# A decode layer on one core: w_down, gate and up dealt over the partitions in another way

## The chip, the core and the metric

The kernel runs on one core of one Trainium2 chip. The metric is the device time of one execution in microseconds (us), the median of several runs. The profile shows one execution on the same chip: what each engine did, what it waited for, and what the DMA queues moved. Engines are called as in the profile: PE is TensorE, DVE is VectorE, ACT is ScalarE, POOL is GpSimd and SP is SyncE. "PEld" is the loading of weights into PE, and "SPq" or "POOLq" is the sequencer of an engine that issues transfers.

## The reference

One token passes a layer norm, and its normalised row feeds attention over a cache of 16384 positions in 32 heads and a gated feed-forward block; both results are added to the token. All is float32.

```python
def _A_ref(x, k_cache, v_cache, wq, wo):
    q = (x @ wq).reshape(B, Sq, H, Dh) ...
    scores = einsum("bhqd,bhkd->bhqk", q, k_cache) * (Dh ** -0.5)
    o = einsum("bhqk,bhkd->bhqd", softmax(scores), v_cache)
    return o ... @ wo

def _B_ref(x, w_gate, w_up, w_down):
    h = gelu(x @ w_gate) * (x @ w_up)
    return h @ w_down

xn = layernorm(x)
return x + _A_ref(xn, ...) + _B_ref(xn, ...)
```

## The kernel before

Nearly all the work is reading: two caches of 268 MB each and 51 MB of weights. SBUF holds three slots of 64 KB a partition: two for keys (`kslot`, lines 62 to 63) and one for values (`vslot`, lines 65 to 66). Every weight and cache tile passes through one of them, and a load waits until the former content of its slot has been used. All loads but those of the token are issued by SP with `load` (lines 68 to 70), in the order of the program.

**Start.** SP loads wq, the fourth rows and the tails of gate and up (lines 74 to 80), then the main part of gate, later that of up (line 169). The token's row is normalised and turned into columns (lines 82 to 126). `project` (lines 128 to 141) multiplies it with a weight matrix: the columns of the result are cut into four quarters, quarter q goes to partitions 32q to 32q+31 of PSUM, and each quarter is cut again into pieces of at most 512 columns, a PSUM bank each. For gate and up a quarter has 4608 / 4 = 1152 columns in pieces of 396, 396 and 360. Each of the five steps (four groups of 128 input rows and a tail of 64 rows) is 12 matmuls. The last 64 input rows lie in halves: the first 2304 columns in one set of partitions, the others in the other.

`ffn` (lines 165 to 179) then brings the result to where w_down needs it: DVE multiplies each piece with `same`, which keeps for every partition the one block of columns that belongs to it, and a reduction adds the blocks. Partition p ends with the 36 values of gate (and of up) that stand for the rows 36p to 36p+35 of w_down. `ffn_act` (lines 186 to 196) makes hT from them, 36 values a partition.

**Heads.** For each head SP loads one tile of keys and one of values (8.4 MB each, 64 KB a partition). DVE multiplies keys by the query and reduces (lines 210 to 216), a softmax follows, and PE multiplies the weights with the values (lines 232 to 237).

**End.** w_down (`wd`) lies with 36 rows a partition, wo with 32. SP loads 28 rows of wd into the value slot when the last but one head's values have been used, 8 rows into the key slot that comes free next together with 16 rows of wo, and 8, 4, 2, 1 and 1 rows of wo into the last slot (lines 287 to 297). A "row" here is 2304 bytes in each of 128 partitions. PE multiplies each row, 288 columns at a time, with one column of hT or oT (`add_out`, lines 278 to 282, called from lines 312 to 325). wd rows come first, then wo rows in the order of their loads. Ahead of the last four wo rows DVE adds the partial sums to the token (lines 320 and 321), PE adds that in (line 324), and after the last row DVE copies the result and ACT stores it (lines 327 to 329).

GpSimd has only a few memsets and an identity matrix at the start and issues no transfer.

Of the kernel before, what the change touches and what calls it, by code (L numbers as in the profile page):

```python
# [19 lines left out]
DM = P * DJ  # L20
# [15 lines left out]
HG = 4  # L36
# [5 lines left out]
def kernel(ctx: ExitStack, tc: tile.TileContext, x, k_cache, v_cache, wq, wo, wg, wu, wd, out):  # L42
    nc = tc.nc
    cpool = ctx.enter_context(tc.tile_pool(name="cpool", bufs=1))
# [12 lines left out]
    wmain = {n: w[:DM].rearrange("(p j) f -> p (j f)", j=DJ) for n, w in (("q", wq), ("g", wg), ("u", wu))}  # L57
    wtail = {n: w[DM:].rearrange("d (s f) -> (d s) f", s=2) for n, w in (("q", wq), ("g", wg), ("u", wu))}
    wov = wo.rearrange("(p t) f -> p (t f)", t=WO_T)
    wdv = wd.rearrange("(p t) f -> p (t f)", t=WD_T)  # L60

    def kslot():
        return kpool.tile([P, R * DH], F32, tag="k", name="kslot")

    def vslot():
        return vpool.tile([P, R * DH], F32, tag="v", name="vslot")

    def load(dst, src):
        nc.sync.dma_start(dst, src)  # L69
# [9 lines left out]
        tails[n] = load(mix[:, at + DF : at + DF + DF // 2], wtail[n])  # L79
        at += DF + DF // 2  # L80

    xrow = mix[:1, ROW3 + FG : ROW3 + FG + D]
    nc.scalar.dma_start(xrow, xf)
    x2 = cpool.tile([P, HALF], F32, name="x2")
    nc.gpsimd.memset(x2, 0.0)
# [11 lines left out]
    same = cpool.tile([P, 32], F32, name="same")  # L97
# [18 lines left out]
    xd = mix[:1, ROW3 + 2 * FG : ROW3 + 2 * FG + 2 * (D - DM)].rearrange("o (d s) -> o d s", s=2)  # L116
# [4 lines left out]
    xnb = cpool.tile([P, DJ, 32], F32, name="xnb")  # L121
# [3 lines left out]
    xtb = cpool.tile([P, 2, 32], F32, name="xtb")  # L125
    nc.vector.tensor_copy(xtb, xt.unsqueeze(2).to_broadcast([P, 2, 32]))

    def project(steps, group, sizes):
        pg = ps_big.tile([P, 3, 512], F32, tag="pb", name="pg")
        for k, (j, rhs) in enumerate(steps):  # L130
            for b, size in enumerate(sizes):
                for q in range(4):
                    lo = q * group + sum(sizes[:b])
                    if j < DJ:
                        lhs = xnb[:, j, :]
                    else:
                        lhs = xtb[:, q // 2, :]
                        lo -= q // 2 * 2 * group
                    nc.tensor.matmul(pg[32 * q : 32 * q + 32, b, :size], lhs, rhs[:, lo : lo + size],  # L139
                                     start=k == 0, stop=k == len(steps) - 1)  # L140
        return pg

    steps = [(DJ, qt)] + [(j, wq_t[:, j * HD : (j + 1) * HD]) for j in range(DJ)]
    pq = project(steps, QG, (QB, QB))[:, :2, :]
# [5 lines left out]
    def q_spread(h):  # L150
        r = 32 * (h // (H // 4))
        lo = h % (H // 4) * DH
        pq = ps_s.tile([P, 512], F32, tag="sm", name="pq")
        nc.tensor.matmul(pq, ones[r : r + 1, :], qrow[r : r + 1, lo : lo + QH * DH], start=True, stop=True)  # L154
        return pq
# [4 lines left out]
        for i in range(QH):  # L160
            Q[h + i] = qs[:, i : i + 1, :]

    gu = cpool.tile([P, 2, WD_T], F32, name="gu")

    def ffn(which):
        n = "gu"[which]
        t = kslot() if which else wg_t
        steps = [(3, row3[n]), (DJ, tails[n])]
        load(t[:, :ROW3], wmain[n][:, :ROW3])
        steps += [(j, t[:, j * DF : (j + 1) * DF]) for j in range(DJ - 1)]  # L170
        pg = project(steps, FG, FB)
        gm = mix[:, ROW3 : ROW3 + FG].rearrange("p (m t) -> p m t", t=WD_T)
        at = 0
        for b, size in enumerate(FB):
            m = size // WD_T
            nc.vector.tensor_mul(gm[:, at : at + m, :], pg[:, b, :size].rearrange("p (m t) -> p m t", t=WD_T),  # L176
                                 same[:, at : at + m].unsqueeze(2).to_broadcast([P, m, WD_T]))
            at += m
        nc.vector.tensor_reduce(gu[:, which, :], gm.rearrange("p m t -> p t m"), axis=AX.X, op=ALU.add)  # L179

    ffn(0)
    ffn(1)

    hT = cpool.tile([P, WD_T], F32, name="hT")

    def ffn_act():
        g, u = gu[:, 0], gu[:, 1]
        t1 = cpool.tile([P, WD_T], F32, name="t1")
# [3 lines left out]
        th = cpool.tile([P, WD_T], F32, name="th")  # L192
        nc.scalar.activation(th, t1, AF.Tanh, scale=0.7978845608028654)
        t2 = cpool.tile([P, WD_T], F32, name="t2")
# [54 lines left out]
    for h in range(H + 1):  # L249
# [7 lines left out]
        pq = q_spread(h + 1) if more else None  # L257
# [20 lines left out]
    def add_out(groups, lhs, w, last=False):  # L278
        n = D // len(groups)
        for i, g in enumerate(groups):  # L280
            nc.tensor.matmul(g, lhs, w[:, i * n : (i + 1) * n], start=id(g) not in seen, stop=last)  # L281
# [29 lines left out]

    for j, w in enumerate(wd_rows):
        add_out(half[j % 2], hT[:, j : j + 1], w)

    for j, w in enumerate(wo_rows):
        if j < WO_T - WO_Q:
# [2 lines left out]
        if j == WO_T - 4:  # L319
            nc.vector.tensor_add(x2[:64], x2[:64], PO[0][64:, :HALF])  # L320
# [37 lines left out]
```

## Time and profile before

| | |
|---|---|
| time, median of 3 runs | 1370.0 us (1369.81 to 1370.03) |
| time of the profiled execution | 1370.16 us |
| its span, first to last instruction | 1368.3 us |
| bytes read | 587.60 MB, 429 GB/s over the span |
| busy share | DVE 83%, PE 30%, PE weight loads 9%, ACT 3%, POOL 0% |
| PE's granted clock, mean | 0.623 of full speed |

The profile's page cuts the span into 40 slices and gives a busy share for each engine and for the 16 DMA engines, lists the DMA queues, follows the chain of work that ended last back to its start, and lists groups of instructions with the busy time, the mean duration, and the idle time before them with the name of what ended it. Other views give the same chain in order of time, the instructions of a stretch one by one, and, for windows of one's choice, the busy time of each engine, the granted clock, the mean busy share of the DMA engines and the rate. The DMA views show no single DMA engine, only the mean of the sixteen.

### The profile page before, as it was taken

Reading aid. Unit: us, or ns where it says so; the run is one execution under the profiler, and the core shown is the slowest. Engines: PE = TensorE matmul, PEld = TensorE weight load, DVE = VectorE, ACT = ScalarE, POOL = GpSimd, SP = SyncE. Lnnn points to the kernel's source line nnn. Section 1 sums busy time; section 2 is a strip of 40 time slices with the busy share of each in tenths; the row PEclk is TensorE's granted clock in tenths of the full one; section 3 lists DMA queues with packets and bytes.
Section 4 is the critical chain, followed back from the end, with each engine's and each line's share of the span. In section 5 each row is a group of like instructions: output and inputs, shape, how many; then the busy total and the mean of one; then the engine's idle time right before and its main releaser. Section 6 shows DMA issues by size and latency. Waiting matters only on the chain.

```text
span 1368.3 us, 6377 instructions
## 1 busy us (share of the span) xinstructions
PE 406.0 (30%) x2870; PEld 118.1 (9%) x2870; DVE 1135.8 (83%) x169; ACT 36.5 (3%) x126; POOL 1.0 (0%) x7
## 2 busy tenths in 40 slices
PE   4321233322311232323212332322213333221156
PEld 1110000100000000100000000100001000000012
DVE  1069999899888888898888888998888888988840
ACT  0000000000000000000000000000000000000000
POOL 0000000000000000000000000000000000000000
PEclk8775565565556556565566566565556555665577
DMA  9999999999999999999999999999999999999997
GB/s 404 440 425 450 430 429 430 430 435 432 437 435 429 431 430 439 432 432 435 431 436 433 433 431 430 435 432 439 435 430 430 431 432 437 438 435 428 429 428 336
DMA packets 11704, 588.00 MB, mean 430 GB/s; under 512 B 1303, under 2 KB 1309, under 8 KB 1694
## 3 DMA queue, kind: packets, MB, share of 16 engines
q1 hardware_dynamic: 11664, 587.60, 99.4%
q8 instruction: 22, 0.36, 0.1%
q14 instruction: 4, 0.03, 0.0%
q10 hardware_dynamic: 14, 0.01, 0.0%
HBM read 587.60 MB, written 0.00 MB: 429 GB/s over the span
## 4 chain that ended last, share of the span: by engine, by line
DMA 51%; DVE 46%; PE 2%; issue 0%; SPq 0%; ACT 0%; DVEq 0%
DMA kslot<-in_A_k_cache_dram 41%; DVE s L216 23%; DVE kslot L215 23%; DMA kslot<-in_A_v_cache_dram 3%; DMA kslot<-in_B_w_up_dram 3%; DMA kslot<-in_A_wo_dram 3%; DMA kslot<-in_A_wq_dram 2%; PE pg L139 1%; PE po L236 1%; DVE gu L179 0%; SPq L69 0%; PE pt L222 0%; DVE vslot L176 0%; DVE pm L220 0%; DVE nm L224 0%
## 5 line engine op out<-in xcount | busy, mean ns | idle before, releaser
L215 DVE TENSOR_TENSOR kslot<-kslot,qs 128x16384 f32<-128x16384 f32 (+1 forms) x33 | 551.3, 16705 | 88.4 <-DMA kslot<-in_A_k_cache_dram 86.9
L216 DVE TENSOR_REDUCE s<-kslot 128x128 f32<-128x16384 f32 (+1 forms) x33 | 551.2, 16703 | 3.3
L236 PE MATMUL po<-vslot,pe 128*16 128x512 f32 x1984 | 286.1, 741 | 645.0 <-DMA vslot<-in_A_v_cache_dram 645.0
L236 PEld LDWEIGHTS po<-vslot,pe 128*16 128x16 f32 x1984 | 67.3, 113 | 848.2 <-issue 848.2
L222 PE MATMUL pt<-ident,pm 128*1 128x128 f32 x32 | 11.9, 372 | 236.0 <-DVE pm L220 236.0
L176 DVE TENSOR_TENSOR vslot<-pg,same 128x396 f32<-128x396 f32 (+1 forms) x6 | 3.0, 552 | 69.1 <-PE pg L139 69.1
L139 PE MATMUL pg<-kslot,xnb 128*32 128x396 f32 (+2 forms) x208 | 23.6, 615 | 33.6 <-DMA kslot<-in_B_w_gate_dram 18.9
L228 ACT ACTIVATE nb<-pb 128x1 f32<-128x1 f32 x32 | 5.5, 171 | 812.4 <-PE pb L226 812.4
L320 DVE TENSOR_TENSOR x<-x,po 64x288 f32<-64x288 f32 x1 | 0.5, 457 | 30.8 <-PE po L281 30.8
L222 PEld LDWEIGHTS pt<-ident,pm 128*1 128x1 f32 x32 | 2.5, 79 | 259.4 <-DVE pm L220 218.5
L226 PE MATMUL pb<-nm,ones 1*128 1x1 f32 x64 | 18.1, 350 | 13.2 <-DVE nm L224 13.2
L224 DVE TENSOR_REDUCE nm<-pt 1x1 f32<-1x128 f32 x32 | 8.9, 278 | 14.9 <-PE pt L222 14.9
L226 PEld LDWEIGHTS pb<-nm,ones 1*128 1x128 f32 x64 | 15.8, 305 | 22.2 <-DVE nm L224 11.3
L154 PE MATMUL pq<-qrow,ones 1*128 1x512 f32 x16 | 15.6, 1073 | 0.0
L229 ACT ACTIVATE pe<-s,nb 128x128 f32<-128x128 f32 x32 | 12.8, 401 | 1.0
L302 DVE RECIPROCAL rl<-pl 128x32 f32<-128x32 f32 x1 | 0.4, 358 | 14.9 <-PE pl L300 14.9
L281 PE MATMUL acc<-kslot,oT 128*1 128x144 f32 (+1 forms) x112 | 10.5, 376 | 6.7 <-DMA kslot<-in_A_wo_dram 6.7
L139 PEld LDWEIGHTS pg<-kslot,xnb 128*32 128x32 f32 x208 | 7.1, 126 | 51.0 <-DMA kslot<-in_B_w_gate_dram 19.7
L241 ACT ACTIVATE o<-po 128x512 f32<-128x512 f32 x8 | 4.8, 597 | 222.0 <-PE po L236 222.0
L236 PE MATMUL po<-kslot,pe 128*16 128x512 f32 x64 | 9.6, 769 | 2.6 <-DMA kslot<-in_A_v_cache_dram 2.6
L281 PE MATMUL acc<-vslot,hT 128*1 128x288 f32 x56 | 8.6, 473 | 5.6 <-DMA vslot<-in_B_w_down_dram 5.6
L245 PE MATMUL pc<-same,o 128*128 128x4 f32 x64 | 8.4, 255 | 5.7 <-ACT o L241 5.7
(74 smaller groups left out, 109.9 us busy)
## 6 DMA issues: line engine op xcount, KB each, us to landing
kslot<-in_A_k_cache_dram SPq DMA_DIRECT2D x2, 4096.0 KB
vslot<-in_B_w_down_dram SPq DMA_DIRECT2D x1, 8064.0 KB
kslot<-in_B_w_gate_dram SPq DMA_DIRECT2D x1, 6912.0 KB, 54.0
kslot<-in_B_w_up_dram SPq DMA_DIRECT2D x1, 6912.0 KB
kslot<-in_A_wo_dram SPq DMA_DIRECT2D x1, 4608.0 KB, 39.2
vslot<-in_B_w_gate_dram SPq DMA_DIRECT2D x1, 2304.0 KB, 28.9
vslot<-in_B_w_up_dram SPq DMA_DIRECT2D x1, 2304.0 KB, 37.6
kslot<-in_B_w_down_dram SPq DMA_DIRECT2D x1, 2304.0 KB, 28.7
```

The source lines that it names most:

```text
L139: nc.tensor.matmul(pg[32 * q : 32 * q + 32, b, :size], lhs, rhs[:, lo : lo + size], start=k == 0, stop=k == len(steps) - 1)
L154: nc.tensor.matmul(pq, ones[r : r + 1, :], qrow[r : r + 1, lo : lo + QH * DH], start=True, stop=True)
L215: tc.keep_in_program_order(nc.vector.tensor_mul(blk, blk, Q[h].to_broadcast([P, n, DH])))
L216: nc.vector.tensor_reduce(S[h][:, i : i + n], blk, axis=AX.X, op=ALU.add)
L222: nc.tensor.transpose(pt[:1, :P], pm, ident)
L224: tc.keep_in_program_order(nc.vector.tensor_reduce(nm, pt[:1, :P], axis=AX.X, op=ALU.max, negate=True))
L226: nc.tensor.matmul(pb[:, :1], ones[:1, :], nm, start=True, stop=True)
L228: nc.scalar.activation(nb, pb[:, :1], AF.Copy, scale=SCALE)
L229: nc.scalar.activation(pe4, S.pop(h).rearrange("p (k s) -> p k s", s=4), AF.Exp, bias=nb, scale=SCALE, accum_out=lsum[:, h : h + 1])
L236: nc.tensor.matmul(PO[h // HG % 2][q : q + PW, :], pe[:, lo : lo + PW], vt[:, k * 512 : (k + 1) * 512], start=i == 0 and k < 4, stop=i == ...
L245: nc.tensor.matmul(pc[:, :HG], o4[:, j * DH : (j + 1) * DH], pick[:, j, :], start=j == 0, stop=j == 3)
L281: nc.tensor.matmul(g, lhs, w[:, i * n : (i + 1) * n], start=id(g) not in seen, stop=last)
```

## The change

w_down is cut in two. Its first 128 x 33 = 4224 rows lie with 33 rows a partition and are loaded by SP as before, 16 rows into the value slot and 17 into the key slot. The last 384 rows lie with 12 rows in each of the partitions 96 to 127. They are loaded by GpSimd into the rest of the value slot, in four transfers: transfer r covers the eight partitions 96+r, 100+r, ..., 124+r, and each partition's 12 rows as two halves of 6 rows (13,824 bytes) with a gap of 8 numbers between them. Ahead of each large transfer GpSimd issues a tiny one of the same form, eight partitions (0, 4, ..., 28) with two pieces of 8 bytes, whose data nobody uses.

Gate and up are cut to match: three quarters have 1056 columns (pieces of 495, 495 and 66), the last has 1056 + 384 = 1440 (495, 495 and 450). A piece of the tail that reaches over column 2304 is multiplied in two parts. `gu`, `hT` and the tiles of the activation get 45 columns instead of 36; `gu` is zeroed first. For the partitions 96 to 127 DVE makes one more product and one more reduction for each of gate and up.

At the end PE multiplies the 33 wd rows, then the 12 extra ones (with 32 partitions each), then the wo rows. wo is loaded in pieces of 11, 5, 8, 4, 2, 1 and 1 rows instead of 16, 8, 4, 2, 1 and 1: 11 rows share the key slot with wd, the others go to the last slot.

The order of instructions on SP is unchanged but for the one more wo transfer; GpSimd gets eight transfers at its end. The eight are issued in program order, each tiny one ahead of its large one; the first of them waits for the release of the value slot, as SP's wd transfer into it does.

```diff
-WD_T = DF // P
-FG = DF // 4
-FB = (11 * WD_T, 11 * WD_T, 10 * WD_T)
+WD_T = 33
+WD_X = 12
+GAP = 8
+XP = 96
+DX = P * WD_T
+FT = WD_T + WD_X
+FG = 32 * WD_T
+FB = (15, 15, 2)
+FX = 32 * WD_X
...
-WD_PIECES = (28, 8)
-WO_PIECES = (16, 8, 4, 2, 1, 1)
-WO_A = 16
+WD_PIECES = (16, 17)
+WO_PIECES = (11, 5, 8, 4, 2, 1, 1)
+WO_A = 11
...
-    wdv = wd.rearrange("(p t) f -> p (t f)", t=WD_T)
+    wdv = wd[:DX].rearrange("(p t) f -> p (t f)", t=WD_T)
+    wdx = wd[DX:].rearrange("(p t) f -> p (t f)", t=WD_X)
...
-    def project(steps, group, sizes):
+    def project(steps, total, bases, sizes):
         pg = ps_big.tile([P, 3, 512], F32, tag="pb", name="pg")
+        h = total // 2
         for k, (j, rhs) in enumerate(steps):
-            for b, size in enumerate(sizes):
+            for b in range(len(sizes[0])):
                 for q in range(4):
-                    lo = q * group + sum(sizes[:b])
+                    lo = bases[q] + sum(sizes[q][:b])
+                    hi = lo + sizes[q][b]
                     if j < DJ:
-                        lhs = xnb[:, j, :]
+                        parts = [(xnb[:, j, :], lo, hi, 0)]
                     else:
-                        lhs = xtb[:, q // 2, :]
-                        lo -= q // 2 * 2 * group
-                    nc.tensor.matmul(pg[32 * q : 32 * q + 32, b, :size], lhs, rhs[:, lo : lo + size],
-                                     start=k == 0, stop=k == len(steps) - 1)
+                        parts = [(xtb[:, i, :], max(lo, i * h), min(hi, i * h + h), i * h) for i in range(2)]
+                    for lhs, a, e, o in parts:
+                        if a < e:
+                            nc.tensor.matmul(pg[32 * q : 32 * q + 32, b, a - lo : e - lo], lhs, rhs[:, a - o : e - o],
+                                             start=k == 0, stop=k == len(steps) - 1)
         return pg
...
-    gu = cpool.tile([P, 2, WD_T], F32, name="gu")
+    gu = cpool.tile([P, 2, FT], F32, name="gu")
+    nc.vector.memset(gu, 0.0)
+    fcols = [tuple(m * WD_T for m in FB)] * 3 + [tuple(m * WD_T + FX * (b == 2) for b, m in enumerate(FB))]
...
-        nc.vector.tensor_reduce(gu[:, which, :], gm.rearrange("p m t -> p t m"), axis=AX.X, op=ALU.add)
+        nc.vector.tensor_reduce(gu[:, which, :WD_T], gm.rearrange("p m t -> p t m"), axis=AX.X, op=ALU.add)
+        gx = mix[XP:, ROW3 + FG : ROW3 + FG + FX].rearrange("p (m t) -> p m t", t=WD_X)
+        nc.vector.tensor_mul(gx, pg[XP:, 2, FB[2] * WD_T : FB[2] * WD_T + FX].rearrange("p (m t) -> p m t", t=WD_X),
+                             same[XP:, :].unsqueeze(2).to_broadcast([32, 32, WD_X]))
+        nc.vector.tensor_reduce(gu[XP:, which, WD_T:], gx.rearrange("p m t -> p t m"), axis=AX.X, op=ALU.add)
...
-    wd_rows = load_rows(ta, 0, wdv, 0, a) + load_rows(tb, 0, wdv, a, b)
+    wd_rows = load_rows(ta, 0, wdv, 0, a)
+    xh = WD_X // 2 * D
+    ext = ta[:, a * D : a * D + 2 * (xh + GAP)].rearrange("p (s f) -> p s f", s=2)
+    at = a * D + 2 * (xh + GAP)
+    tiny = ta[0:32:4, at : at + 32].rearrange("p (r s f) -> p r s f", r=4, s=2)
+    for r in range(4):
+        src = wdx[r::4, :].rearrange("p (s f) -> p s f", s=2)
+        tc.keep_in_program_order(nc.gpsimd.dma_start(tiny[:, r, :, :2], src[:, :, :2]))
+        tc.keep_in_program_order(nc.gpsimd.dma_start(ext[XP + r : P : 4, :, :xh], src))
+    wd_rows += load_rows(tb, 0, wdv, a, b)
+    wd_x = [ext[XP:, s, j * D : (j + 1) * D] for s in range(2) for j in range(WD_X // 2)]
...
     for j, w in enumerate(wd_rows):
         add_out(half[j % 2], hT[:, j : j + 1], w)
+    for j, w in enumerate(wd_x):
+        add_out(half[j % 2], hT[XP:, WD_T + j : WD_T + j + 1], w)
```

More of the change, by code (lines that the diff above doesn't have):

```diff
@@ L80 @@
         at += DF + DF // 2
-    xrow = mix[:1, ROW3 + FG : ROW3 + FG + D]
+    XAT = ROW3 + FG + FX
+    xrow = mix[:1, XAT : XAT + D]
     nc.scalar.dma_start(xrow, xf)
@@ L115 @@
         nc.tensor.matmul(px[:, j : j + 1], xm[:, j, :], ones[:1, :1], start=True, stop=True)
-    xd = mix[:1, ROW3 + 2 * FG : ROW3 + 2 * FG + 2 * (D - DM)].rearrange("o (d s) -> o d s", s=2)
+    xd = mix[:1, XAT + D : XAT + D + 2 * (D - DM)].rearrange("o (d s) -> o d s", s=2)
     nc.vector.tensor_copy(xd, xrow[:, DM:].unsqueeze(2).to_broadcast([1, D - DM, 2]))
@@ L170, in ffn @@
         steps += [(j, t[:, j * DF : (j + 1) * DF]) for j in range(DJ - 1)]
-        pg = project(steps, FG, FB)
+        pg = project(steps, DF, [q * FG for q in range(4)], fcols)
         gm = mix[:, ROW3 : ROW3 + FG].rearrange("p (m t) -> p m t", t=WD_T)
         at = 0
-        for b, size in enumerate(FB):
-            m = size // WD_T
-            nc.vector.tensor_mul(gm[:, at : at + m, :], pg[:, b, :size].rearrange("p (m t) -> p m t", t=WD_T),
+        for b, m in enumerate(FB):
+            nc.vector.tensor_mul(gm[:, at : at + m, :], pg[:, b, : m * WD_T].rearrange("p (m t) -> p m t", t=WD_T),
                                  same[:, at : at + m].unsqueeze(2).to_broadcast([P, m, WD_T]))
             at += m
-        nc.vector.tensor_reduce(gu[:, which, :], gm.rearrange("p m t -> p t m"), axis=AX.X, op=ALU.add)
+        nc.vector.tensor_reduce(gu[:, which, :WD_T], gm.rearrange("p m t -> p t m"), axis=AX.X, op=ALU.add)
[3 more added lines that the diff above has]
+        nc.vector.tensor_reduce(gu[XP:, which, WD_T:], gx.rearrange("p m t -> p t m"), axis=AX.X, op=ALU.add)
     ffn(0)
     ffn(1)
-    hT = cpool.tile([P, WD_T], F32, name="hT")
+    hT = cpool.tile([P, FT], F32, name="hT")
     def ffn_act():
         g, u = gu[:, 0], gu[:, 1]
-        t1 = cpool.tile([P, WD_T], F32, name="t1")
+        t1 = cpool.tile([P, FT], F32, name="t1")
         tc.keep_in_program_order(nc.vector.tensor_mul(t1, g, g))
@@ L191, in ffn_act @@
         tc.keep_in_program_order(nc.vector.tensor_mul(t1, t1, g))
-        th = cpool.tile([P, WD_T], F32, name="th")
+        th = cpool.tile([P, FT], F32, name="th")
         nc.scalar.activation(th, t1, AF.Tanh, scale=0.7978845608028654)
-        t2 = cpool.tile([P, WD_T], F32, name="t2")
+        t2 = cpool.tile([P, FT], F32, name="t2")
         tc.keep_in_program_order(nc.vector.scalar_tensor_tensor(t2, th, 1.0, g, op0=ALU.add, op1=ALU.mult))
```

2 lines of the change are left out of this document (1 added, 1 removed).

## The prediction

> **What bounds the kernel now.** I read the profile's page first, then the chain of waits, then the windows over the last microseconds, and last the timeline at the two places that the change touches.
>
> ```profile
> span 1368.3 us, 6377 instructions
> ...
> DMA  9999999999999999999999999999999999999997
> ...
> DMA packets 11704, 588.00 MB, mean 430 GB/s; under 512 B 1303, under 2 KB 1309, under 8 KB 1694
> ...
> q1 hardware_dynamic: 11664, 587.60, 99.4%
> q8 instruction: 22, 0.36, 0.1%
> ...
> DMA 51%; DVE 46%; PE 2%; issue 0%; SPq 0%; ACT 0%; DVEq 0%
> ...
> L215 DVE TENSOR_TENSOR kslot<-kslot,qs 128x16384 f32<-128x16384 f32 (+1 forms) x33 | 551.3, 16705 | 88.4 <-DMA kslot<-in_A_k_cache_dram 86.9
> ```
>
> The DMA engines are busy in every slice but the last. Queue q1, SP's, fills 99.4% of sixteen engines: 0.994 x 16 x 1368.3 = 21,761 engine-us for 587.60 MB, so one engine moves 27.0 KB/us. The chain's 46% for VectorE looks like a second bound, but VectorE itself waited 86.9 us for keys: it has slack and follows the transfers. So the time is the time at which the slowest of sixteen DMA engines finishes, and a short tail behind it. The chain in order of time shows that tail:
>
> ```profile
> 1275.26 42.84 DMA kslot<-in_A_v_cache_dram
> ...
> 1318.24 9.66 PE po L236 x64
> ...
> 1329.71 35.08 DMA kslot<-in_A_wo_dram
> ...
> 1364.83 0.47 PE acc L281 x8
> 1365.32 0.31 DVE kslot L328
> ```
>
> The last V lands at 1318.1 and is used up by 1327.9, and the last row of wo is awaited until 1364.78; 3.5 us of matmuls, copy and store follow to the span's end, and 1.9 us lie around the span (1370.16 for this execution, 1370.0 the median of the runs). What the sixteen engines do in that end is seen in windows of 1 us; behind the busy times of the engines stand TensorE's granted clock, the DMA engines' mean busy share, and GB/s:
>
> ```profile
> 1358.00:1359.00 1.00, 1.00 (x20) 0.38 (x16) 0.00 (x0) 0.00 (x0) 0.00 (x0) 1.00 0.95 383
> 1359.00:1360.00 1.00, 1.00 (x24) 0.40 (x20) 0.00 (x0) 0.00 (x0) 0.00 (x0) 1.00 0.82 316
> 1360.00:1361.00 1.00, 1.00 (x24) 0.41 (x20) 0.00 (x0) 0.00 (x0) 0.00 (x0) 1.00 0.58 228
> 1361.00:1362.00 1.00, 0.61 (x12) 0.06 (x5) 0.32 (x1) 0.00 (x0) 0.00 (x0) 1.00 0.52 203
> 1362.00:1363.00 1.00, 0.98 (x32) 0.74 (x32) 0.58 (x2) 0.00 (x0) 0.00 (x0) 1.00 0.43 171
> 1363.00:1364.00 1.00, 1.00 (x32) 0.41 (x24) 0.00 (x0) 0.00 (x0) 0.00 (x0) 1.00 0.37 138
> 1364.00:1365.00 1.00, 0.70 (x21) 0.21 (x16) 0.00 (x0) 0.00 (x0) 0.00 (x0) 1.00 0.04 16
> ```
>
> This is the view that matters. The share falls to one half by 1361, stays there for a microsecond and a half, and then falls to nothing: about eight engines are done early, eight late. The part above 0.5 from 1359 on sums to 0.32 + 0.08 + 0.02 = 0.42 us of sixteen engines, 0.84 us for each of eight: the early half ends at 1359.8 in the mean, its last engine at about 1361.3 (0.02 x 16 = 0.3 us into that window). The late half ends at 1359 + 2 x (0.5 + 0.5 + 0.5 + 0.43 + 0.37 + 0.04) = 1363.7 in the mean, its last at about 1364.4. The halves are 3.9 us apart. No view says which engines are late.
>
> **The change, part by part.** (1) Bytes. SP's wd transfers lose three rows of 2304 B in each of 128 partitions, 884,736 B, spread over sixteen engines like the rest of q1: 55.3 KB, 55.3 / 27.0 = 2.05 us less on each. The same bytes come back as four GpSimd transfers of eight partitions. If they reach eight engines, each of those gets 110.6 KB, 4.10 us at q1's rate: net 2.05 us later, the other eight 2.05 us earlier. That is just over half of the 3.9 us between the halves, so with the extra bytes on the early half both end together: the early half at 1361.9 in the mean, its last at 1363.4; the late half at 1361.7, its last at 1362.4. The last landing then moves by between 1364.4 - 1363.4 = 1.0 and 2.05 us, the first if the early half's straggler is still that far back. I take **-1.2**, near the straggler's end.
>
> How eight partitions are dealt is no row of this trace. The Trainium skill, "DMA: Bandwidth & Descriptors", section "Why a DMA increments its semaphore by 16 and not by 1", says that a GpSimd transfer of eight partitions uses eight consecutive engines from a round-robin cursor; tiny transfers ahead would then step the cursor so that all four large ones fall on the same eight, and the sum is the one above or its mirror image, by the half. The same section names an exception in which some direct copies go to the lowest-numbered engines without the cursor, and the section "Rules for kernel authors" says that splitting by partition halves is not worth it, since both halves spray over all sixteen; by that the sum would be zero.
>
> (2) Queues. SP's wd transfer into the V slot and GpSimd's eight wait for the same release:
>
> ```profile
> 1308.00 0.33 SPq L69 DMA_DIRECT2D vslot<-in_B_w_down_dram  x1
> ...
> 1314.35 15.79 SPq L69 DMA_DIRECT2D kslot<-in_A_wo_dram  x6
> ```
>
> So GpSimd starts near 1308 and has nothing else to do. Its issue costs stand in no row: SP's 0.33 us is the low end, and the high end is when TensorE first needs the extra rows, about 1347 (below), 39 us later. Up to that they cost nothing. The large transfers delay the last V (in flight until 1318) by up to 4.1 us on their engines, so the release for the last wo tile slips from 1328 to at most 1332; SP has 28 rows queued in the slot before, until about 1349, which hides it.
>
> (3) Gate and up. The quarters become 1056, 1056, 1056 and 1440 columns.
>
> ```profile
> 59.59 8.13 PE L139 MATMUL pg<-kslot,xnb 128*32 128x396 f32 x72 [18.88 <-DMA kslot<-in_B_w_gate_dram]
> 67.79 14.66 SPq L69 DMA_DIRECT2D kslot<-in_A_k_cache_dram  x3
> ...
> 76.05 6.01 PE L139 MATMUL pg<-kslot,xnb 128*32 128x396 f32 x72 [2.58 <-DMA kslot<-in_B_w_up_dram]
> 82.13 1.49 DVE L176 TENSOR_TENSOR vslot<-pg,same 128x396 f32<-128x396 f32 x3 [10.57 <-PE pg L139]
> 83.65 2.17 DVE L179 TENSOR_REDUCE gu<-vslot 128x36 f32<-128x1152 f32 x1
> 85.84 0.33 SPq L69 DMA_DIRECT2D vslot<-in_A_v_cache_dram  x1
> ```
>
> If four quarters run side by side, the longest sets the time: 1440 / 1152, a quarter more; if by total columns, nothing more. So gate's 8.13 us grow by 0 to 2.0, up's 6.01 by 0 to 1.5. VectorE adds a product and a reduction over 384 columns: a third of 1.49 and of 2.17, less a twelfth of each for the shorter main part, about 1 us each time. All of it is hidden: the first key load moves from 67.79 to at most 69.8, while up's weights stream until 76; the first V load from 85.84 to at most 88.4, while the first keys (8.4 MB, 19 us at 430 GB/s) stream until 95. VectorE starts head 0 up to 2.5 us later and has 86.9 us of waiting to make it good in. Without that cover it would cost those 2.5 us. I put **0**; the memset of gu and nine more columns in the activation are hidden by the same.
>
> (4) TensorE's tail. The rows are 45 + 32 instead of 36 + 32, and wo comes in 11, 5, 8, 4, 2, 1, 1.
>
> ```profile
> 1347.32 0.41 PE L281 MATMUL po<-kslot,hT 128*1 128x288 f32 x2
> ...
> 1356.56 0.69 PE L281 MATMUL acc<-kslot,oT 128*1 128x288 f32 x2
> ...
> 1357.04 0.68 PE L281 MATMUL acc<-kslot,oT 128*1 128x288 f32 x2
> ...
> 1358.04 0.41 PE L281 MATMUL acc<-kslot,oT 128*1 128x288 f32 x2
> ...
> 1358.28 0.41 PE L281 MATMUL acc<-kslot,oT 128*1 128x288 f32 x2
> ...
> 1361.68 0.46 DVE L320 TENSOR_TENSOR x<-x,po 64x288 f32<-64x288 f32 x1 [30.80 <-PE po L281]
> 1362.02 1.16 PE L281 MATMUL acc<-kslot,oT 128*1 128x144 f32 x32 [0.41 <-DMA kslot<-in_A_wo_dram]
> ...
> 1363.11 0.42 PE L324 MATMUL acc<-x,ones 1*1 1x144 f32 x8
> 1363.46 1.06 PE L281 MATMUL acc<-kslot,oT 128*1 128x144 f32 x24
> 1364.83 0.42 PE L281 MATMUL acc<-kslot,oT 128*1 128x144 f32 x8 [0.30 <-DMA kslot<-in_A_wo_dram]
> ```
>
> A row takes 0.48 us at the half clock, 0.24 at the full one. Counted back from the last landing E at 18.4 KB an engine and row (0.68 us), wd's 17 rows land at E-21.8, wo's at E-14.3, E-10.9, E-5.5 and on. From E-21.8, 45 rows (17 + 12 + 11 + 5), eight of them slow, take 3.8 + 8.9 us, to E-9.1. TensorE then idles 3.6 us. What an idle does to the clock is seen ahead of wo, where the last matmul of wd ended at 1347.73:
>
> ```profile
> 1350.00:1351.00 1.00, 0.00 (x0) 0.00 (x0) 0.00 (x0) 0.00 (x0) 0.00 (x0) 0.87 0.90 387
> 1351.00:1353.00 2.00, 0.00 (x0) 0.00 (x0) 0.00 (x0) 0.00 (x0) 0.00 (x0) 0.50 0.97 415
> ```
>
> It fell 3.0 us after. (The Trainium skill, "TensorE: Matmul & The Clock Gate", warns of gaps of over about 3 us; this row agrees.) If it falls, the eight rows end at E-1.6 instead of E-3.2 as now; four rows (1.16), the sums (0.42), three rows (1.06) and the last (0.42) follow to E+1.4 against E+0.5: 0.9 us. If it holds, 0; if it stays low to the end, the four pieces double and it is 4. I take **+0.5**.
>
> **Sum**: 1370.16 - 1.2 + 0 + 0.5 = 1369.5 against this execution, 1369.3 against the median.
>
> **Rivals.**
> - *The extra bytes fall on late engines*, all eight or some of them. Nothing in the profile names the half. Then the latest end at 1364.4 + 2.05, and with the tail 1370.0 + 2.05 + 0.5 = 1372.5 (1372.0 to 1373.0): slower. It decides as soon as one of the latest engines is among the eight.
> - *The extra bytes spread over all sixteen*: the change deals nothing anew, 1370.0 + 0.5 = 1370.5.
> - *A second queue costs its engine more than its bytes.* For it speaks q8: 22 packets of 16.4 KB take 0.1% (0.05 to 0.15) of 21,893 engine-us, 0.5 to 1.5 us each, against 0.61 at q1's rate. By its middle, 1.0 us, 110.6 KB cost 6.7 us instead of 4.1: the early half's last ends at 1361.3 - 2.05 + 6.7 = 1366.0, 1.6 later than now, 1372.1 in all; by its high end, 10.1 us, 1375.5. It decides from 5.2 us for those bytes. Against it: q8's packets go elsewhere than to the tiles.
>
> **Chances.** The forecast 0.48, late engines 0.28, all sixteen 0.12, dear packets 0.12. The likeliest is 1369.3. The range reaches from 1368.2 (the full 2.05 and no tail) to 1373.0, the end of the first rival; dear packets beyond it are left out. A measurement here tells about 0.2%, 2.7 us, from no change. Faster than 1367.3: 0.03, since even full balance gives 2. Slower than 1372.7: part of the first rival and half of the last, 0.2. Within: 0.77.
>
> **What will show it.** In windows over the last microseconds the share of the DMA engines should fall from full to nothing in some 2 us with no plateau at one half. With late engines the plateau gets longer, to some 8 us; with all sixteen it stays. A GpSimd queue should show 0.88 MB, and its share of sixteen engines 0.15% at q1's rate, 0.25% or more if its packets are dear. The key and value stretch, 39 us a head (16.8 MB at 430 GB/s), should not move; if the DMA share dips below one near 70 or 90 us, step 3 is wrong. If TensorE shows no wait for the last wo row and the clock reads 0.50 after wo's five rows, the tail is the bound, not the transfers.

## The result and the profile after

The changed kernel takes **1390.0 us** (median of 4 runs, 1388.1 to 1390.5) against 1370.0 us (1369.8 to 1370.1) before: 1.0143 times as long, with a 95% interval of 1.0126 to 1.0161. The prediction was 1369.3 in a range of 1368.2 to 1373.0. The profiled execution took 1389.7 us.

The page of the changed kernel, with the queues (packets, MB, share of sixteen engines) and the chain's shares:

```profile
span 1387.9 us, 6480 instructions
...
q1 hardware_dynamic: 11808, 586.72, 97.7%
q0 software_dynamic: 320, 0.89, 0.2%
...
DMA 47%; DVE 45%; PE 5%; another core or an unknown queue 1%; issue 0%; ACT 0%; SPq 0%; DVEq 0%
```

The bytes are what the prediction said: 0.88 MB have gone from q1 to GpSimd's queue q0, which fills 0.2% of sixteen engines. That lies between the forecast's two values, 0.15% at q1's rate and 0.25% for dear packets; the packets themselves decide below. PE now holds 5% of the chain instead of 2%. The timeline of the end shows where:

```profile
1304.46 0.33 SPq L76 DMA_DIRECT2D vslot<-in_B_w_down_dram  x1
...
1314.61 5.32 PE L252 MATMUL po<-kslot,pe 128*16 128x512 f32 x24 [2.47 <-DMA kslot<-in_A_v_cache_dram]
...
1326.35 0.69 POOL L316 DMA_DIRECT2D vslot<-in_B_w_down_dram  x1 [1324.77 <-PE pl L326]
...
1330.37 0.56 POOL L317 DMA_DIRECT2D vslot<-in_B_w_down_dram  x1
...
1360.32 2.10 PE L297 MATMUL acc<-kslot,oT 128*1 128x144 f32 x32 [32.24 <-DMA kslot<-in_A_wo_dram]
1362.19 0.69 PE L297 MATMUL acc<-vslot,hT 128*1 128x288 f32 x2
...
1384.89 0.31 DVE L356 COPY kslot<-acc 128x144 f32<-128x144 f32 x1 [1.63 <-PE acc L297]
```

Read the shapes in the fifth row: 128x144 is a quarter-width row of wo, one of the last eight (four rows are 16 matmuls, and the trace lists each twice, x32). Before the change those came last. Now the four of the piece of 4 are the first part of the output that PE computes, 32 us after its work before, and only behind them does the first wd row follow (vslot, hT). The transfers are long over by then, as the windows show (PE's busy time first, then the other engines; the last three numbers are PE's granted clock, the DMA engines' busy share and GB/s):

```profile
1355.00:1360.00 5.00, 0.00 (x0) 0.00 (x0) 0.00 (x0) 0.00 (x0) 0.00 (x0) 0.50 0.57 237
1360.00:1365.00 5.00, 4.68 (x64) 2.13 (x68) 0.00 (x0) 0.00 (x0) 0.00 (x0) 0.57 0.15 56
1365.00:1370.00 5.00, 5.00 (x88) 1.92 (x84) 0.00 (x0) 0.00 (x0) 0.00 (x0) 1.00 0.00 0
```

The last 25 us of the kernel are matmuls that, behind that one wait, wait for no transfer; SP's 16 wd rows had been there since 1326 and were used from 1362 on. Two more things differ from the forecast. GpSimd did not start at the release of the V slot, as "The change" above and the prediction have it (SP's transfer at 1304.46), but at 1326.35, 22 us later; the name behind its wait, a matmul of PE, only happens to end then. And the last V landed at 1314.6 instead of 1318.2, though nothing in the heads was touched.

The built programs, the lists of instructions of each engine with what each waits for, give the first two. In the changed one the 16 quarter-width matmuls (line 297) stand on PE right behind the transpose of line 334, ahead of all rows of wd; in the one before they stand last. GpSimd's first transfer waits for the landing of SP's 16 rows in the same tile, and the first wd row for all four large GpSimd transfers, though neither touches the other's bytes. If the slices are written as eight consecutive partitions instead of every fourth one, both waits and the new order are gone from the built program.

### The profile page after: what moved, and what is told of

Same layout as the page of the kernel before. It is cut to its first block, busy times and chain, and to the rows that moved or that the text cites. A ratio compares the mean times of both kernels' runs of the same rounds, so it can differ in the third digit from the quotient of the medians.

```text
span 1387.9 us, 6480 instructions
## 1 busy us (share of the span) xinstructions
PE 411.1 (30%) x2910; PEld 122.1 (9%) x2910; DVE 1138.4 (82%) x174; ACT 36.6 (3%) x126; POOL 5.5 (0%) x15
## 4 chain that ended last, share of the span: by engine, by line
DMA 47%; DVE 45%; PE 5%; another core or an unknown queue 1%; issue 0%; ACT 0%; SPq 0%; DVEq 0%
DMA kslot<-in_A_k_cache_dram 40%; DVE s L232 22%; DVE kslot L231 22%; DMA kslot<-in_A_v_cache_dram 3%; PE pg L150 3%; DMA kslot<-in_A_wo_dram 3%; DMA kslot<-in_A_wq_dram 2%; PE acc L297 2%; PE po L252 1%; DVE gu L191 0%; PE pt L238 0%; DVE vslot L188 0%; SPq L76 0%; DVE pm L236 0%
## 5 line engine op out<-in xcount | busy, mean ns | idle before, releaser
L188 DVE TENSOR_TENSOR vslot<-pg,same 128x495 f32<-128x495 f32 (+1 forms) x6 | 2.8, 516 | 68.9 <-PE pg L150 68.9
L150 PE MATMUL pg<-kslot,xnb 128*32 128x495 f32 (+3 forms) x208 | 27.4, 623 | 29.3 <-DMA kslot<-in_B_w_gate_dram 17.4
L236 DVE TENSOR_REDUCE pm<-s 128x1 f32<-128x128 f32 x32 | 9.2, 286 | 1.1
```

Source lines behind the costliest of these rows:

```text
L150: nc.tensor.matmul(pg[32 * q : 32 * q + 32, b, a - lo : e - lo], lhs, rhs[:, a - o : e - o], start=k == 0, stop=k == len(steps) - 1)
L236: tc.keep_in_program_order(nc.vector.reduce_max(pm, S[h], axis=AX.X))
```

## The experiments

All times are medians; every ratio is against the kernel before on the same chip.

### 1. Hold TensorE's order: order_kept

```diff
-            nc.tensor.matmul(g, lhs, w[:, i * n : (i + 1) * n], start=id(g) not in seen, stop=last)
+            tc.keep_in_program_order(nc.tensor.matmul(g, lhs, w[:, i * n : (i + 1) * n], start=id(g) not in seen, stop=last))
```

> The changed kernel with the output rows of TensorE held in the order in which the program writes them; nothing else. Theory A (the 20 us are TensorE's order: the four quarter-width rows of the wo piece of four stand ahead of all of wd's rows, so 33 + 12 + 24 rows start only when that piece lands, at 1360): wd's rows go first. By the semaphores they still wait for all four large GpSimd transfers, whose last packet lands at 1350.7 in the changed kernel, so TensorE's tail runs from about 1351 to about 1376 in place of 1360 to 1385, and the time is 1380 to 1382. Rival B (the transfers themselves, dear packets or late engines, cost the 20 us): the time stays near 1390, and the trace shows TensorE waiting for a row that lands late.

Measured: **1378.8 us**, ratio 1.0063 (1.0048 to 1.0078). Timeline of its end:

```profile
1326.72 0.69 POOL L316 DMA_DIRECT2D vslot<-in_B_w_down_dram  x1 [1325.15 <-DVE kslot L332]
...
1351.35 0.65 PE L297 MATMUL acc<-vslot,hT 128*1 128x288 f32 x2 [24.14 <-DMA vslot<-in_B_w_down_dram]
...
1373.59 0.31 DVE L356 COPY kslot<-acc 128x144 f32<-128x144 f32 x1 [1.63 <-PE acc L297]
```

The order alone was worth 11.2 us, a little more than theory A had (1380 to 1382). The first row is a wd row now, and it starts at 1351.35, though SP's 16 rows were there before GpSimd's first transfer at 1326.7: it waited for GpSimd's last landing, as theory A said. From there all rows run without a wait for any transfer; PE, not the transfers, ends the kernel.

### 2. Eight consecutive partitions: eight_consecutive and eight_late

```diff
-    tiny = ta[0:32:4, at : at + 32].rearrange("p (r s f) -> p r s f", r=4, s=2)
+    tiny = ta[0:8, at : at + 32].rearrange("p (r s f) -> p r s f", r=4, s=2)
...
-        src = wdx[r::4, :].rearrange("p (s f) -> p s f", s=2)
+        src = wdx[8 * r : 8 * r + 8, :].rearrange("p (s f) -> p s f", s=2)
...
-        tc.keep_in_program_order(nc.gpsimd.dma_start(ext[XP + r : P : 4, :, :xh], src))
+        tc.keep_in_program_order(nc.gpsimd.dma_start(ext[XP + 8 * r : XP + 8 * r + 8, :, :xh], src))
```

> The changed kernel with each GpSimd transfer on eight consecutive partitions (96 to 103, and so on) in place of every fourth one; the rows of wd that a partition holds are dealt to match, the order on TensorE is free. Same transfers, same bytes. Theory A (the slices with a step of four over the partitions make the program wait as if each touched the whole tile: GpSimd for SP's 16 rows, TensorE's first wd row for all GpSimd transfers, and that wait makes the scheduler put the wo piece of four ahead): GpSimd issues near 1304, TensorE starts wd's rows near 1326 to 1330, the quarter-width rows come last again, and the time is 1368 to 1371, set by the last landing. Rival B (the transfers cost the 20 us): near 1390.

Measured: **1382.4 us**, ratio 1.0089 (1.0074 to 1.0104). Neither number came. Its timeline:

```profile
1305.94 0.69 POOL L316 DMA_DIRECT2D vslot<-in_B_w_down_dram  x1 [1304.36 <-PE po L252]
...
1333.38 0.65 PE L297 MATMUL acc<-vslot,hT 128*1 128x288 f32 x2 [3.44 <-DMA vslot<-in_B_w_down_dram]
...
1375.87 0.42 PE L297 MATMUL acc<-kslot,oT 128*1 128x144 f32 x8 [0.28 <-DMA kslot<-in_A_wo_dram]
```

Here is the shape that the prediction had in mind: GpSimd starts at the release (1305.9), wd's rows come first, the last row of wo last, after a wait for the last landing. But that landing is at 1375.9. The windows of the same kernel say why:

```profile
1310.00:1315.00 5.00, 0.95 (x3) 0.57 (x3) 1.41 (x3) 0.66 (x3) 0.51 (x1) 0.50 0.99 333
...
1325.00:1330.00 5.00, 3.06 (x24) 1.81 (x16) 0.84 (x3) 0.80 (x3) 0.00 (x0) 0.88 0.97 271
...
1345.00:1350.00 5.00, 0.00 (x0) 0.00 (x0) 0.00 (x0) 0.00 (x0) 0.00 (x0) 0.50 0.93 220
...
1355.00:1360.00 5.00, 5.00 (x52) 1.63 (x48) 0.00 (x0) 0.00 (x0) 0.00 (x0) 0.55 0.99 424
```

A busy share of one is no proof of full speed. As long as GpSimd's transfers are in flight the engines are as busy as ever and move 220 to 333 GB/s in these windows; afterwards 424. The trace's records of single packets, which no view lists, agree: GpSimd's packets of 13,824 bytes took 774 ns in the median and up to 1611, where each of the 64 took 516 ns in the changed kernel, and SP's packets beside them stretched as well (36,864 bytes: 1638 instead of 1364 ns in the median). Is it the moment, among the last V and the first wd rows, or the place? The second kernel adds one line to it:

```diff
+    tc.keep_in_program_order(nc.gpsimd.tensor_copy(ta[:, at + 64 : at + 65], ta[:, a * D - 1 : a * D]))
```

> The kernel of eight consecutive partitions with GpSimd held back by one small copy that reads the last of SP's 16 wd rows in the V slot, so that its transfers start near 1326 as in the changed kernel and not at 1306 among the last V and the first wd rows. Theory P (eight engines that write into eight neighbouring partitions get in each other's way and stop SP's packets behind them): packets of 13,824 bytes still take 700 ns and more, SP's pieces beside them stretch by 20 to 30%, and the time is 1378 to 1384. Rival T (only the moment is bad, because GpSimd's transfers collide with the V and wd loads): 516 ns, last landing near 1363, 1368 to 1370.

Measured: **1396.4 us**, ratio 1.0191 (1.0176 to 1.0207), above both. Two rows tell the two parts of it, a window and an instruction:

```profile
1355.00:1360.00 5.00, 0.00 (x0) 0.00 (x0) 0.00 (x0) 0.00 (x0) 0.00 (x0) 0.50 0.99 230
```

```profile
1373.31 2.10 PE L297 MATMUL acc<-kslot,oT 128*1 128x144 f32 x32 [24.18 <-DMA kslot<-in_A_wo_dram]
```

The transfers are slow at the later moment too (230 GB/s at a share of 0.99; 845 ns a packet), so it is not the moment, and rival T falls. And the quarter-width rows are ahead again, here of the extra rows and of the other wo rows, with a wait of 24.2 us, which the expectation had not foreseen: the order on PE came back with a wait put elsewhere. Why the scheduler orders them so, no run shows.

### 3. Keep every fourth partition and put the V slot's rows last: slot_a_last

PE's rows are held in order, as in experiment 1, and the order is another: the second slot's rows first.

```diff
-    for j, w in enumerate(wd_rows):
+    for j, w in enumerate(wd_rows[a:]):
+        add_out(half[j % 2], hT[:, a + j : a + j + 1], w)
+    for j, w in enumerate(wo_rows[:WO_A]):
+        add_out(half[j % 2], oT[:, j : j + 1], w)
+    for j, w in enumerate(wd_rows[:a]):
         add_out(half[j % 2], hT[:, j : j + 1], w)
...
     for j, w in enumerate(wo_rows):
+        if j < WO_A:
+            continue
```

> The changed kernel, its transfers and their layout (every fourth partition) untouched, with the output rows of TensorE held in another order: first the 17 wd rows and 11 wo rows of the second slot, then the 16 wd rows and 12 extra rows of the V slot, which wait for the GpSimd transfers, then the other wo rows. Theory A (all of the 20 us is TensorE's order): rows run from 1338 on, the V slot's 28 rows from 1351 to 1360, the last row waits for the last landing near 1363, and the time is 1367.5 to 1369.5. Rival B (the transfers themselves cost something beyond their 2 us on late engines): above 1371.

Measured: **1370.1 us**, ratio 0.9998 (0.9988 to 1.0008): between the two numbers, 20 us under the changed kernel with the very same transfers. Timeline, then windows:

```profile
1338.64 0.65 PE L297 MATMUL acc<-kslot,hT 128*1 128x288 f32 x2 [9.96 <-DMA kslot<-in_B_w_down_dram]
...
1348.14 0.65 PE L297 MATMUL acc<-kslot,oT 128*1 128x288 f32 x2 [3.74 <-DMA kslot<-in_A_wo_dram]
...
1365.81 0.31 DVE L362 COPY kslot<-acc 128x144 f32<-128x144 f32 x1 [1.63 <-PE acc L297]
```

```profile
1359.00:1360.00 1.00, 1.00 (x20) 0.31 (x16) 0.00 (x0) 0.00 (x0) 0.00 (x0) 1.00 0.37 157
...
1361.00:1362.00 1.00, 1.00 (x24) 0.42 (x16) 0.00 (x0) 0.00 (x0) 0.00 (x0) 1.00 0.35 141
1362.00:1363.00 1.00, 1.00 (x24) 0.51 (x18) 0.00 (x0) 0.00 (x0) 0.00 (x0) 1.00 0.31 122
1363.00:1364.00 1.00, 1.00 (x30) 0.67 (x22) 0.73 (x2) 0.00 (x0) 0.00 (x0) 1.00 0.03 12
```

Two things are to be seen. PE is busy without a gap from 1348.14 to 1365.8, so it ends the kernel here too, by a little. And the DMA share stays near 0.35 from 1359 to 1363: 0.35 x 16 = 5.6 engines work on alone, the plateau that the prediction named for its rival of late engines (it said some 8 us). In windows of 0.1 us the share is 0.07 up to 1363.2 and 0.00 behind it, so the last landing is at 1363.2.

### 4. Which engines, and whose partitions: slot_a_last_swap and swap_low32

The first kernel only swaps the two lines in which GpSimd issues the tiny and the large transfer; the second also changes the partitions.

```diff
-        tc.keep_in_program_order(nc.gpsimd.dma_start(tiny[:, r, :, :2], src[:, :, :2]))
         tc.keep_in_program_order(nc.gpsimd.dma_start(ext[XP + r : P : 4, :, :xh], src))
+        tc.keep_in_program_order(nc.gpsimd.dma_start(tiny[:, r, :, :2], src[:, :, :2]))
```

> The kernel of slot_a_last with each large GpSimd transfer issued ahead of its tiny one, which moves the large ones to the other eight engines; the partitions stay every fourth one from 96 on. Theory P (an engine that writes into the partitions that another engine is writing at that moment slows both; in the changed kernel each engine's extra partitions are its own): the packets of 13,824 bytes take 700 to 1100 ns in place of 516, SP's packets beside them stretch by a third, the last landing is 5 to 15 us later, 1373 to 1384. Rival Q (the engine does not matter to the partition): 516 ns, and since the other eight hold only two of the late engines, between 2 us less than slot_a_last and the same.

Measured: **1377.5 us**, ratio 1.0050 (1.0035 to 1.0065). Three of its windows, while GpSimd's transfers are in flight:

```profile
1330.00:1335.00 5.00, 0.00 (x0) 0.00 (x0) 0.00 (x0) 0.00 (x0) 1.39 (x3) 0.50 0.95 288
...
1345.00:1350.00 5.00, 0.82 (x12) 0.10 (x4) 0.00 (x0) 0.00 (x0) 0.00 (x0) 0.95 0.99 269
1350.00:1355.00 5.00, 2.97 (x28) 1.02 (x32) 0.00 (x0) 0.00 (x0) 0.00 (x0) 0.50 1.01 277
```

The same rates as with eight neighbouring partitions, at a share of one; a packet of 13,824 bytes took 787 ns in the median. Two lines in the other order cost 7.4 us.

```diff
-        tc.keep_in_program_order(nc.gpsimd.dma_start(ext[XP + r : P : 4, :, :xh], src))
+        tc.keep_in_program_order(nc.gpsimd.dma_start(ext[r:32:4, :, :xh], src))
...
-    wd_x = [ext[XP:, s, j * D : (j + 1) * D] for s in range(2) for j in range(WD_X // 2)]
+    wd_x = [ext[:32, s, j * D : (j + 1) * D] for s in range(2) for j in range(WD_X // 2)]
...
-        add_out(half[j % 2], hT[XP:, WD_T + j : WD_T + j + 1], w)
+        add_out(half[j % 2], hT[:32, WD_T + j : WD_T + j + 1], w)
```

> The kernel of slot_a_last_swap with the extra rows written to partitions 0 to 31 (every fourth one) in place of 96 to 127; they meet zeros there, so the products of the extra rows are left out of the output, with every instruction kept. Theory P (an engine is slow only where it writes into partitions that belong to another engine, and the first eight engines own 0 to 31): the packets of 13,824 bytes take 516 ns again, the last landing is 1361.5 to 1363.6, the time 1368 to 1370.2. Rival S (the other eight engines are slow for GpSimd's packets wherever they write): 787 ns as in slot_a_last_swap, and the time near 1377.

Measured: **1368.6 us**, ratio 0.9992 (0.9982 to 1.0002). One window in flight, then the end:

```profile
1345.00:1350.00 5.00, 3.58 (x56) 1.49 (x60) 0.00 (x0) 0.00 (x0) 0.00 (x0) 1.00 1.00 425
...
1358.00:1359.00 1.00, 1.00 (x23) 0.42 (x16) 0.00 (x0) 0.00 (x0) 0.00 (x0) 1.00 0.72 283
1359.00:1360.00 1.00, 0.94 (x12) 0.18 (x4) 0.01 (x1) 0.00 (x0) 0.00 (x0) 1.00 0.21 85
1360.00:1361.00 1.00, 0.58 (x20) 0.54 (x24) 0.89 (x2) 0.00 (x0) 0.00 (x0) 1.00 0.12 48
```

425 GB/s, and each of the 64 packets took 516 ns again. The same engines are slow in one place and not in the other, and the same place is slow for one set of engines and not for the other. So an engine's packets are slow where it writes into partitions that another engine writes, and the change had matched the two: its tiny transfers turn the large ones to the engines that own the partitions 96 to 127. No view names the engine of a packet; that is inferred from these kernels and from their plateaus, and the fourth combination, the engines of the change in the partitions 0 to 31, was not run. The Trainium skill, "DMA: Bandwidth & Descriptors", section "The descriptor swizzle", gives such a table, four neighbouring partitions (and their like 32 further on) to an engine, the first eight engines for 0 to 63; these runs agree with it.

The second thing is the end: here the share falls from 0.72 to 0.21 within 1359, and 0.12 x 16 = 2 engines go on, where 5.6 did in slot_a_last. Among the eight engines of the change there are about six of the late ones, among the other eight about two.

### 5. What the extra bytes cost: no_extra_rows

```diff
-        tc.keep_in_program_order(nc.gpsimd.dma_start(ext[XP + r : P : 4, :, :xh], src))
...
-    for j, w in enumerate(wd_x):
-        add_out(half[j % 2], hT[XP:, WD_T + j : WD_T + j + 1], w)
```

> The kernel of slot_a_last without the four large GpSimd transfers and without the 12 rows that they bring: the products of the last 1,536 rows... of wd are left out of the output, the tiny transfers stay. It measures what the 0.88 MB cost at the end. Theory L (six of the eight engines that carry them are among the last to finish): the last landing, 1363.5 in slot_a_last, comes 4.1 us earlier, near 1359.4, and the time, with TensorE's 12 rows (2.9 us) gone as well, is 1366 to 1367. Rival E (they were carried by engines that are done early): the last landing stays within 0.5 us of 1363.5 and the time above 1368.5.

(The text says 1,536 rows of wd; the 12 rows in 32 partitions are 384.) Measured: **1364.7 us**, ratio 0.9960 (0.9945 to 0.9975), lower than expected because PE now ends right behind the last landing:

```profile
1359.22 0.43 PE L297 MATMUL acc<-kslot,oT 128*1 128x144 f32 x8 [0.28 <-DMA kslot<-in_A_wo_dram]
```

The last packets land at 1358.9, by windows of 0.1 us, instead of 1363.2: 4.3 us for 110.6 KB an engine, against 4.10 in the prediction. The engines that finish last carry the extra bytes. Theory L holds.

### 6. The start of the slots: five kernels

That the last V came some 3.5 us earlier after the change has nothing to do with its purpose. The three slots lie behind the small tiles, and these have grown: in the built programs the first slot starts at 27,680 bytes before and at 27,904 after, the others 64 and 128 KB further on. Four kernels pad or shorten the small tiles of the kernel before; eight_consecutive_32off pads the kernel of eight consecutive partitions.

```diff
+    pad = cpool.tile([P, 8], F32, name="pad")
```

with 8, 24 or 56 numbers, and for 512 bytes:

```diff
-    std = cpool.tile([1, 1], F32, name="std")
+    sr = cpool.tile([1, 2], F32, name="sr")
+    std, rstd = sr[:, :1], sr[:, 1:]
...
-    rstd = cpool.tile([1, 1], F32, name="rstd")
```

> The kernel before with eight floats a partition more ahead of the key, V and wd slots, so that the slots start at 27,712, 93,248 and 158,784 bytes, multiples of 64, in place of 32 past such multiples. Theory C (the start of the slots sets the pace): 19.32 us a key tile in place of 19.36, the last V lands near 1314.5 in place of 1318.1, and the time is 1366.0 to 1367.0. Rival D (the pace comes from something else): 1369.5 to 1370.5.

> The kernel of eight consecutive partitions with eight more floats a partition ahead of the key, V and wd slots, which puts each slot's start 32 bytes further (27,936 in place of 27,904, and so on). Theory C (the start of the slots sets the pace of the stream: 19.32 us a key tile at starts that are multiples of 64 bytes, 19.36 at 32 past one): last V 3 to 4 us later, and the time 3 to 4 us over eight_consecutive. Rival D (the pace is of the chip or of the run, or comes with another part of the change): equal to eight_consecutive within 1 us.

> The kernel before with 24 floats a partition more: slots at 27,776, 93,312 and 158,848 bytes, multiples of 128 and not of 256. So far starts 32 past a multiple of 64 gave 1370.1, multiples of 64 1369.5, of 256 1366.6. If 256 is needed, 1369 to 1369.6; if 128 is enough, 1366.4 to 1366.8.

> The kernel before with 56 floats a partition more, so that the slots start where those of the changed kernel start: 27,904, 93,440 and 158,976 bytes, multiples of 256 (the step of 32 bytes gave only 0.6 us, its starts being multiples of 64). Theory C2 (the start of the slots sets the pace, and a multiple of 256 is needed): 19.32 us a key tile, last V near 1314.5, 1366.0 to 1367.0. Rival D (the changed kernel's pace comes from something else in it, such as its instruction loads): 1369.3 to 1370.2.

> The kernel before with two one-number tiles merged into one, which takes 32 bytes away ahead of the slots: they start at 27,648, 93,184 and 158,720 bytes, multiples of 512. If what counts is a multiple of 256, as 1366.6 at 27,904 says, the time is 1366.2 to 1366.9, with nothing padded. If a larger multiple helps further, the key tile falls below 19.32 us and the time below 1366. If the 1366.6 was the padding's (another place of the other tiles), it stays at 1370.

| kernel | first slot starts at | time, us | ratio to before |
|---|---|---|---|
| before | 27,680, 32 past a multiple of 64 | 1370.1 | |
| before_32on | 27,712, a multiple of 64 | 1369.5 | 0.9995 (0.9986 to 1.0005) |
| before_128on | 27,776, of 128 | 1369.3 | 0.9993 (0.9984 to 1.0003) |
| before_256on | 27,904, of 256 | **1366.6** | 0.9974 (0.9963 to 0.9984) |
| before_512on | 27,648, of 512 | **1366.7** | 0.9976 (0.9967 to 0.9985) |
| eight_consecutive_32off | 27,936 | 1385.2, against 1382.4 at 27,904 | 1.0110 (1.0094 to 1.0127) |

The landing of the last V, as the first matmul that waited for it, in the kernels at multiples of 64, 256 and 512:

```profile
1317.50 2.76 PE L237 MATMUL po<-kslot,pe 128*16 128x512 f32 x12 [2.56 <-DMA kslot<-in_A_v_cache_dram]
```

```profile
1315.05 5.29 PE L237 MATMUL po<-kslot,pe 128*16 128x512 f32 x32 [2.51 <-DMA kslot<-in_A_v_cache_dram]
```

```profile
1315.03 5.56 PE L236 MATMUL po<-kslot,pe 128*16 128x512 f32 x33 [2.46 <-DMA kslot<-in_A_v_cache_dram]
```

Theory C held in its second form only: multiples of 64 and 128 bring 0.6 and 0.8 us, not clear of noise by their intervals, a multiple of 256 brings 3.5, and 512 nothing more. before_512on has smaller tiles ahead of the slots than the kernel before and gives the same as before_256on, so it is the start and not the padding. In the kernel of eight consecutive partitions 32 bytes cost 2.8 us, a little less than expected. before_256on and before_512on beat both the kernel before and the changed one. The Trainium skill, "DMA: Bandwidth & Descriptors", section "How a descriptor splits into AXI transactions", says that a transaction must start at a multiple of 256 bytes, and that for a descriptor which starts elsewhere the first one begins at the boundary below and the unused bytes still cost. It says so of bytes that are fetched, where here the place written starts off the multiple. The step between 128 and 256 agrees, and the size is the runs': 3.5 us over 588 MB.

The end of before_256on serves as the measure for slot_a_last, which has the same starts:

```profile
1360.00:1361.00 1.00, 0.91 (x28) 0.50 (x28) 0.14 (x1) 0.00 (x0) 0.00 (x0) 1.00 0.24 95
1361.00:1362.00 1.00, 0.74 (x24) 0.23 (x15) 0.19 (x1) 0.00 (x0) 0.00 (x0) 1.00 0.00 0
```

```profile
1361.81 0.31 DVE L329 COPY kslot<-acc 128x144 f32<-128x144 f32 x1 [1.67 <-PE acc L282]
```

Its last landing is at about 1361.0, and the copy of the result 0.8 us behind it.

## Why the prediction was wrong, point by point

The 20 us, taken apart by neighbouring kernels. The second pair differs in the whole new deal, each of the others in one thing:

| from, to | what | us |
|---|---|---|
| before, before_256on | slots start at a multiple of 256 bytes | 1370.1 - 3.5 = 1366.6 |
| before_256on, slot_a_last | the new deal itself: extra bytes on late engines, and PE's later rows | + 3.5 = 1370.1 |
| slot_a_last, order_kept | the V slot's rows come first, and PE can't start before GpSimd's last landing | + 8.7 = 1378.8 |
| order_kept, changed kernel | the quarter-width wo rows stand ahead of wd | + 11.2 = 1390.0 |

**Step 4, TensorE's tail, failed.** "From E-21.8, 45 rows (17 + 12 + 11 + 5), eight of them slow, take 3.8 + 8.9 us" took the rows in the order of the program and their start from the landing of their own bytes. Neither is given. The order on PE is the scheduler's wherever it isn't held, and the wait for a row is for all that the program believes to touch its tile. A tail put at +0.5 us grew by 20, 11.2 by the order (experiment 1) and 8.7 by the wait (3). That the slices with a step over the partitions cause the wait is shown by the two built programs and by GpSimd's start (1326.35 against 1305.94); by what rule they do it was only argued. The prediction's last sign came nearest: it named a tail of PE as the bound, with the wait for a wo row in another place than it thought.

**Step 2, queues, failed** in its start: "GpSimd starts near 1308 and has nothing else to do". It had to wait for SP's 16 rows. Its cost was put at nothing up to 1347, when PE would first need the extra rows; by the built program PE had to have them before its first wd row, and they landed at about 1351 (order_kept).

**Step 1, bytes, was right in size and wrong in place.** 4.10 us for eight engines were measured as 4.3, but of the eight about six are late ones and not early ones. The prediction had no reason for the early half; it said itself that no view names the late engines, and why these finish late stays open. The last landing moved by 1363.2 - 1361.0 = +2.2 us (at equal slot starts) instead of -1.2; the rival of late engines, at 0.28, had +2.05 and the plateau. That rival's 1372.5 is not what slot_a_last shows because the slot starts gave 3.5 us back: without them it would stand near 1373.6. The rest is PE's rows. In the two profiled executions the copy comes 1365.8 - 1361.8 = 4.0 us later than in before_256on: 2.2 for the landing, and 1.8 because PE ends 2.6 us behind the landing in place of 0.8. As PE had no gap after 1348.14, an earlier last landing alone would not have shortened slot_a_last; no run separates the two parts.

**Step 3, gate and up, held.** In the changed kernel gate's matmuls, the first key load, up's matmuls and the first V load are these:

```profile
58.93 9.87 PE L150 MATMUL pg<-kslot,xnb 128*32 128x495 f32 x72 [17.41 <-DMA kslot<-in_B_w_gate_dram]
68.83 14.76 SPq L76 DMA_DIRECT2D kslot<-in_A_k_cache_dram  x3
...
75.67 7.57 PE L150 MATMUL pg<-kslot,xnb 128*32 128x495 f32 x69
...
88.18 0.33 SPq L76 DMA_DIRECT2D vslot<-in_A_v_cache_dram  x1
```

Gate grew by 1.7 us (0 to 2.0 were allowed) and up by 1.6 or a little more, as three of its matmuls stand in another row (0 to 1.5), the key load came 1.0 and the V load 2.3 us later, and nothing of it reached the end: the last V lands at 1314.6, and at 1315.05 in before_256on, which has the same slot starts and the old gate and up. The stretch of the heads was to stay as it is; it became shorter, which no step had in it.

**Dear packets** of a second queue fell: 516 ns for 13,824 bytes is 26.8 KB/us, q1's 27.0. They would have been dear on other engines (787 ns) or in neighbouring partitions (774), which the prediction did not weigh.

## What to carry to other kernels

Read the order and the waits of the built program before pricing a tail: a slice with a step over partitions, written by one queue into a tile that another queue fills, can make every reader of the tile wait for both and push the rows behind them about. A DMA share of one with fewer GB/s than elsewhere meant, here, engines that get in each other's way; look at the two numbers together. Before dealing bytes anew for two microseconds, see that the big buffers start at a multiple of 256 bytes: here that gave 3.5 us for a pad of 224 bytes a partition, or for 32 bytes fewer.

## What the hardware showed that was not expected

- An engine that writes into partitions of another engine (inferred in experiment 4) slows both: 220 to 333 GB/s at a busy share of 0.93 to 1.01 in the windows above, 0.88 MB costing 7.4 us (slot_a_last_swap) to some 12 (eight_consecutive, last packets at 1375.5 against 1363.2).
- GpSimd's transfers of eight partitions go to eight engines in turn, as far as the end of the transfers tells (5.6 engines left over in slot_a_last, 2 in swap_low32): a tiny transfer ahead or behind decides which, and with that 7.4 us.
- The start of a 64 KB buffer costs 0.26% of a stream of 588 MB if it isn't a multiple of 256 bytes; 32, 64 and 128 are nearly alike (1370.1, 1369.5, 1369.3 against 1366.6).
